# Pairing blocks in the gate's convolution, three common PSUM slots, and a new order of instructions

## The chip, the cores and the metric

The kernel runs on one core of a Trainium2 chip. The metric is the device time of one execution in microseconds (us); lower is better. Three runs of the kernel before gave 912.4, 908.27 and 912.25 us, so the median is 912.25 us. The profile is of one further execution of 914.14 us, whose span from the first to the last instruction is 912.2 us.

The engines are named as in the profile. PE is the matrix engine (TensorE), PEld its weight loads, DVE the vector engine, ACT the scalar engine, POOL is GpSimd, and SP is the engine that issues most of the transfers. PSUM is the memory into which PE writes; here it holds eight banks of 512 fp32 words for each of 128 partitions.

## The reference

The input x has 8 batches of 3200 positions and 256 channels. First comes a filter in the frequency domain, then a gated convolution:

```
X = rfft(x, axis=1);  Xr, Xi = X.real, X.imag
Yr = Xr @ w_r - Xi @ w_i + b_r
Yi = Xr @ w_i + Xi @ w_r + b_i
Yr, Yi = soft_threshold(Yr, 0.01), soft_threshold(Yi, 0.01)
y = irfft(Yr + 1j*Yi, n=3200, axis=1)

gate_pre[:, s] = sum over k of conv_w[k] * y[:, s - 4 + k]     (k = 0..4, zeros ahead of s = 0)
gate = 1 / (1 + exp(-gate_pre))
out  = (gate * (y @ w_val)) @ w_out
```

w_val, conv_w and w_out arrive as 64-bit floats; the kernel turns their bit patterns into fp32 with integer instructions on DVE.

## The kernel before

The transform of length 3200 = 64 x 50 is done as two small matrix products each way. For a batch b the stages are:

- p1 (lines 502 to 579): eight units. Each loads a part of x, multiplies it by a 50-point matrix on PE into a two-bank PSUM tile, adds and subtracts the two halves (a copy on ACT, two operations on DVE, L545 and L551), and stores the result to a scratch tensor in HBM (a_dram).
- p2 (lines 582 to 701) with mixed (703 to 749): six steps of two units and one last step of one unit. Each step loads a part of a_dram, does the 64-point product (s2, L610) into a two-bank PSUM tile, splits it on ACT and DVE into a high and a low part, does the complex product with the weights (L734 and L729, with a sum that DVE writes into PSUM first, called the seed, L738), the soft threshold (ACT L745, DVE L747), and the inverse 64-point product (s1i, L681), and stores to a second scratch tensor (z_dram).
- positions (763 to 808): eight blocks of 400 positions. Each loads a part of z_dram, does the inverse 50-point product (s2i, L787) into a two-bank PSUM tile, and ACT copies it (L794) into y_sb, the one buffer that holds y of a whole batch. Block 7 comes first in every batch, since its last positions are also the ones ahead of block 0 in the layout; three small DVE copies (L800, L806) put them there. It has to wait until the last readers of the batch before are done.
- gated (822 to 887): for each of the eight blocks the values v = y @ w_val (L819 in six fp32r products per half from a high and a low part; or L815 with whole fp32 weights, for the blocks in LATE_VAL), the convolution, the sigmoid, the gate (L861), the output product (L819 or, for the blocks in LATE_OUT, L815), a copy (L885) and the store.

The convolution of one block is done for two channel halves c of 128 channels and 400 positions each. ACT multiplies by the first tap (L846), DVE adds four taps (L849, one scalar_tensor_tensor for each tap and half, each with a [128, 1] operand from cw_sb), and ACT applies the sigmoid in place (L859). In a block of LATE_OUT the output product reads the gated values as they are; in the other blocks ACT and DVE split them first (L332 and L334), and the value product's operand y is split in the same way unless the block is in LATE_VAL.

PSUM is divided as follows: one two-bank slot for the tiles of s2 (tag ps_s2), two two-bank slots that all of p1, s1i, s2i, v and the output product take in turn (tag ps_2), and one bank each for the seed's target (ps_y) and the sum (ps_k).

The order of the instructions is worked out before the launch by the class Plan. Every piece of work is given an engine, a cost, the things it reads and writes, the slots it opens, and a due value `at` (in units: a batch is T = 13). Plan.order then simulates the engines in time. On each engine it takes, among the pieces that could begin within SLACK ns of the earliest, the one of the smallest `at`. What comes out is a fixed order on each engine; the constants in LAND, CLOCK and LANDED (before: a plain 1400) are times that only this simulation uses, and O holds the offsets of the due values. At run time every engine works through its list and waits where an operand or a slot isn't there yet. The slots of one tag are taken in the order of their opening, so the n-th tile of a tag with three slots waits for the last reader of tile n - 3.

Of the kernel before, what the change touches and what calls it, by code (L numbers as in the profile page):

```python
# [11 lines left out]
F32R = mybir.dt.float32r  # L12
# [3 lines left out]
ALU = mybir.AluOpType  # L16
# [76 lines left out]
class Plan:  # L93
# [30 lines left out]
    def order(self):  # L124
# [41 lines left out]
        while len(done) < len(pieces):  # L166
# [71 lines left out]
def act(n, kind="copy"):  # L238
# [7 lines left out]
T = float(NU)  # L246
O = {'spread': -0.013,
     'hold': 0.011,
     'together': 2.151,
     'later': 4.433,  # L250
     'load_x': -2.271,
     'p1': 1.18,
     'p1_step': 1.113,
     'load_a': -3.981,
     's2': -1.406,
     's1i': 1.995,
     'p3': 3.283,
     'load_z': -3.105,
     'y': 0.708,
     'conv': 1.374,  # L260
     'val': 1.657,
     'gate': -2.568,
     'project': 3.372,
     'late_val': 7.023,
     'late_out': 14.484,
     'turn': 0.534,
     'mix_sum': -1.534,
     'p1_1': -0.107,
     'load_x_1': 1.103,
     'p1_2': -1.656,  # L270
     'p3_0': 0.32}
# [9 lines left out]
def fourier_filter_then_gated_conv(ctx: ExitStack, tc: tile.TileContext, x, w_r, w_i, b_r, b_i,  # L281
# [34 lines left out]
    WORDS = {"xs": 3072, "x": 4 * D, "zl": MB * D, "y_hl": 4 * TB, "g_hl": 4 * TB, "s1": 1024, "tp": 2 * D, "o": 2 * TB, "acc": 2 * TB}  # L316

# [4 lines left out]
    def two_banks(key, tag="ps_2"):  # L322
        return buffer(key, tag, [P, 2, 512])
# [112 lines left out]
    def load_bias(at):  # L436
# [15 lines left out]
        def spread():  # L452
            p, q = two_banks(k2, "ps_s2")[:, :, 0:D], buffer(k1, "ps_k", [P, D])
            for k in range(2):
                b = b_sb[0:1, k * D:(k + 1) * D]
                for j in range(2):
                    nc.tensor.matmul(p[:, k, :], m(j), b, start=j == 0, stop=j == 1)
# [44 lines left out]
    def p1(b, u, at):  # L502
# [4 lines left out]
        s_tag = ("s1", "g_hl", "xs")[u % 3] if early else "s1"  # L507
        p_tag = "ps_s2" if early and u % 3 == 2 else "ps_2"
        rows = ROWS if b < 2 else ((0, N2),)
# [72 lines left out]
    def p2(b, d, at):  # L582
# [14 lines left out]
        def s2(i):  # L597
            if i == 0:
                two_banks(k2, "ps_s2")
            if last:  # L600
# [155 lines left out]
    def block(ap):  # L756
        return ap.rearrange("p (h n) -> p h n", h=NH)
# [52 lines left out]
    def matrix(key, e, w, src, whole):  # L810
# [6 lines left out]
        for c in range(2):  # L817
            for hw, hy in ((0, 0), (1, 0), (0, 1)):
                nc.tensor.matmul(p[:, e, 0:TB], w[:, hw, c, e * P:(e + 1) * P], src(hy, c), start=n == 0, stop=n == 5)  # L819
                n += 1  # L820

    def gated(b, k, at):
        bk = (b, k)
        here, there = [("y", k, 0)], [("y", k - 1, j) for j in range(3 if k == 0 else 1)]
        ky, kg, kv, kh, kp, ko = (("y_hl", bk), ("acc", bk), ("v_ps", bk), ("gated", bk), ("o_ps", bk), ("o", bk))
        if bk in LATE_VAL:
# [12 lines left out]

        acc = lambda c: tl[kg][:, c, :]  # L840

        def first(c):
            if c == 0:
                buffer(kg, "acc", [P, 2 * TB])
                tl[kg] = tl[kg].rearrange("p (c n) -> p c n", c=2)
            nc.scalar.mul(block(acc(c)), y_at(k, c, 0), cw_sb[:, c, 0:1])  # L846

        def tap(c, j):
            nc.vector.scalar_tensor_tensor(out=block(acc(c)), in0=y_at(k, c, j), scalar=cw_sb[:, c, j:j + 1],  # L849
                                           in1=block(acc(c)), op0=ALU.mult, op1=ALU.add)  # L850
        for c in range(2):
            add(at + O["conv"] + 0.01 * c, "ACT", act(TB, "conv"), lambda c=c: first(c), [*here, *there, ("cw", 0, 0)],
                [kg + (c,)], {kg: "acc"} if c == 0 else None, chain="conv")
        for j in range(1, KC):
            for c in range(2):
                add(at + O["conv"] + 0.02 * j, "DVE", 61 + dve(TB), lambda c=c, j=j: tap(c, j), [*here, *there], [kg + (c,), *([("turn", "read", (b, c))] if (k, j) == (NB - 1, KC - 1) else [])],
                    delay=545 + (130 if j == KC - 1 else 0))
        for c in range(2):
            add(at + O["conv"] + 0.15, "ACT", act(TB, "sigmoid"), lambda c=c: nc.scalar.activation(  # L859
                out=acc(c), in_=acc(c), func=AF.Sigmoid), (), [kg + (c,)])  # L860
        add(at + O["gate"], "DVE", dve(2 * TB), lambda: nc.vector.tensor_tensor(  # L861
            out=tl[kg], in0=tl[kv][:, :, 0:TB], in1=tl[kg], op=ALU.mult), [kv + (0,), kv + (1,)], [kg + (0,), kg + (1,)])
        if bk in LATE_OUT:
            gs = [kg + (0,), ("w_late", 0, 0)]
            om = lambda e: matrix(kp, e, lambda: w_late[1], lambda h, c: tl[kg][:, c, :], True)
        else:
            gs = [*split(at + O["gate"] + 0.1, 2 * TB, kh, lambda: tl[kg], lambda: tl[kh][:, 0], lambda: tl[kh][:, 1],
                         [kg + (0,)], {kh: "g_hl"}, lambda: buffer(kh, "g_hl", [P, 2, 2, TB], F32R)),
                  ("w", "w_out", "high"), ("w", "w_out", "low")]
            om = lambda e: matrix(kp, e, wo_sb, lambda h, c: tl[kh][:, h, c, :], False)  # L870
# [74 lines left out]
    for b in range(B):  # L945
# [44 lines left out]
```

## Time and profile before

| | us |
|---|---|
| median of three runs | 912.25 |
| profiled execution | 914.14 |
| its span | 912.2 |
| outside the span | 1.9 |
| PE busy / idle within the span | 843.4 / 68.8 |
| DVE busy | 798.9 |
| ACT busy | 584.3 |
| granted TensorE clock, mean | 0.971 |

A group's row gives line, engine, operation, out<-in, shapes and count, then the total busy time in us and the mean of one in ns, then the idle time of the engine ahead of it and what ended it. The mean is that of the instruction alone; instructions of one engine overlap a little, so in a run of like ones the distance from start to start is shorter. A row of waits reads: engine, line of what waited, what it waited for, total us, times, longest us. A row of a timeline gives start and length of a run of like instructions (x count) and, in brackets, the idle time ahead of it.

### The profile page before, as it was taken

What the parts mean: (1) busy time and instruction counts of PE and PEld (TensorE: products, weight loads), DVE (VectorE), ACT (ScalarE), POOL (GpSimd) and SP (SyncE); (2) the same over time, 40 slices, a digit from 0 to 9 for tenths busy, and PEclk for the clock granted to TensorE, in tenths of its full rate; (3) what the DMA queues carried; (4) which work ended last, traced back from release to release, by engine and by line L of the source; (5) the groups of instructions that cost most, each with busy time, mean ns of one, the idle gap of its engine ahead of it and who ended that gap; (6) DMA issues with size and microseconds to landing.
All of it is one profiled execution on the core that took longest, in us unless ns stands there. A gap on an engine that the chain in (4) does not pass through costs nothing.

```text
span 912.2 us, 29342 instructions
## 1 busy us (share of the span) xinstructions
PE 843.4 (92%) x12634; PEld 713.5 (78%) x12634; DVE 798.9 (88%) x1286; ACT 584.3 (64%) x903; POOL 4.5 (0%) x11
## 2 busy tenths in 40 slices
PE   8768988999999997999999998899999999999997
PEld 2356766799788886979888887879887888998774
DVE  2347778999999999899999999799999989999896
ACT  1225444778577774768667775768667667777664
POOL 0000000000000000000000000000001000000000
PEclk9779988999999999999999999999999999999999
DMA  6598986764666647655586647656585445523612
GB/s 170 152 218 210 258 228 207 218 202 131 203 210 205 181 128 239 182 195 157 179 251 210 180 138 238 187 192 169 171 253 183 126 132 171 158 79 107 199 69 78
DMA packets 107220, 163.33 MB, mean 179 GB/s; under 512 B 10302, under 2 KB 80756, under 8 KB 107092
## 3 DMA queue, kind: packets, MB, share of 16 engines
q1 hardware_dynamic: 105332, 158.19, 57.4%
q10 hardware_dynamic: 1760, 3.28, 1.3%
q8 instruction: 99, 1.62, 0.8%
q14 instruction: 29, 0.24, 0.1%
HBM read 82.79 MB, written 78.64 MB: 177 GB/s over the span
## 4 chain that ended last, share of the span: by engine, by line
PE 56%; DVE 20%; DMA 13%; ACT 5%; issue 4%; SPq 2%; ACTq 0%; DVEq 0%
PE y_ps L729 10%; PE v_ps L819 10%; PE o_ps L819 10%; PE z_ps L681 7%; DVE acc L849 6%; PE k_ps L734 5%; PE y_p L787 5%; DMA a_dram<-s 5%; DMA x<-in_x 3%; DVE s L551 3%; PE s L610 3%; DMA zl<-z_dram 2%; PE p L532 2%; DVE y_ps L738 2%; DVE acc L861 2%
## 5 line engine op out<-in xcount | busy, mean ns | idle before, releaser
L849 DVE SCALAR_TENSOR_TENSOR acc<-y_sb,cw_sb,acc 128x400 f32<-128x400 f32 x512 | 297.4, 630 | 1.6 <-ACT acc L846 1.2
L729 PE MATMUL y_ps<-w_sb,xs 128*128 128x256 f32 x1152 | 159.3, 289 | 3.7 <-DVE st_cw L374 2.9
L729 PEld LDWEIGHTS y_ps<-w_sb,xs 128*128 128x128 f32 x1152 | 149.1, 196 | 7.8 <-issue 5.4
L819 PE MATMUL o_ps<-gated,wo_sb 128*128 128x400 f32 x744 | 148.5, 347 | 0.0
L819 PE MATMUL v_ps<-y_hl,wv_sb 128*128 128x400 f32 x660 | 133.1, 348 | 9.4 <-DVE s L551 7.3
L819 PEld LDWEIGHTS o_ps<-gated,wo_sb 128*128 128x128 f32 x744 | 134.6, 188 | 2.4
L819 PEld LDWEIGHTS v_ps<-y_hl,wv_sb 128*128 128x128 f32 x660 | 117.2, 189 | 12.4 <-ACT tp L745 4.8
L551 DVE TENSOR_TENSOR s<-p,s 128x512 f32<-128x512 f32 (+2 forms) x144 | 89.6, 627 | 30.8 <-ACT s L545 16.9
L745 ACT ACTIVATE tp<-y_ps,nlam 128x512 f32<-128x512 f32 (+1 forms) x104 | 69.6, 669 | 69.8 <-PE y_ps L729 67.9
L734 PE MATMUL k_ps<-w_sb,xs 128*128 128x256 f32 x576 | 92.9, 298 | 15.7 <-DVE y_ps L738 13.3
L734 PEld LDWEIGHTS k_ps<-w_sb,xs 128*128 128x128 f32 x576 | 77.3, 193 | 33.5 <-issue 14.3
L681 PE MATMUL z_ps<-tp,g_sb 64*64 64x256 f32 x1536 | 95.0, 380 | 3.0 <-issue 1.7
L747 DVE SCALAR_TENSOR_TENSOR tp<-y_ps,tp 128x512 f32<-128x512 f32 (+1 forms) x104 | 69.2, 665 | 24.1 <-ACT tp L745 23.6
L332 ACT CAST gated<-acc 128x800 fp32r<-128x800 f32 x62 | 53.5, 862 | 53.5 <-DVE acc L861 52.6
L787 PEld LDWEIGHTS y_p<-g_sb,zl 50*64 50x64 f32 x4096 | 67.6, 137 | 25.0 <-issue 13.2
L787 PE MATMUL y_p<-g_sb,zl 50*64 50x50 f32 x4096 | 73.0, 221 | 11.9 <-issue 9.4
L846 ACT ACTIVATE acc<-y_sb,cw_sb 128x400 f32<-128x400 f32 x128 | 75.8, 626 | 7.1 <-DVE gated L334 6.2
L610 PEld LDWEIGHTS s<-f_sb,a 64*64 64x64 f32 x3072 | 59.2, 139 | 26.9 <-issue 17.1
L681 PEld LDWEIGHTS z_ps<-tp,g_sb 64*64 64x64 f32 x1536 | 57.3, 133 | 28.9 <-issue 6.7
L532 PE MATMUL p<-x,f_sb 50*64 50x512 f32 x256 | 73.1, 662 | 3.4 <-DMA x<-in_x 2.3
L859 ACT ACTIVATE acc<-acc 128x400 f32<-128x400 f32 x128 | 66.8, 538 | 12.0 <-DVE acc L849 11.8
L794 ACT COPY y_sb<-y_p 128x800 f32<-128x800 f32 x64 | 52.9, 827 | 32.2 <-PE y_p L787 32.0
(80 smaller groups left out, 1046.5 us busy)
## 6 DMA issues: line engine op xcount, KB each, us to landing
zl<-z_dram SPq DMA_DIRECT2D x128, 200.0 KB
out<-o SPq DMA_DIRECT2D x63, 400.0 KB
a<-a_dram SPq DMA_DIRECT2D x96, 256.0 KB
z_dram<-z_t SPq DMA_DIRECT2D x48, 512.0 KB
x<-in_x SPq DMA_DIRECT2D x90, 200.0 KB
a_dram<-s SPq DMA_DIRECT2D x90, 200.0 KB
x<-in_x SPq DMA_DIRECT2D x23, 192.0 KB
a_dram<-s SPq DMA_DIRECT2D x15, 192.0 KB
```

The costliest lines, as they stand in the source:

```text
L532: nc.tensor.matmul(p[k * HP:(k + 1) * HP, 0, :], f1_sb[half(0), 0:HP], xt[half(0), k * 512:(k + 1) * 512], start=True, stop=True)
L551: nc.vector.tensor_tensor(out=st()[lo:hi, h, n], in0=tl[kp][lo:hi, 0, n], in1=st()[lo:hi, 1, n], op=(ALU.add, ALU.subtract)[h])
L610: nc.tensor.matmul(p[e * HP:(e + 1) * HP, h, c, t, :], tl[ka][rows, t, c * P + e * HP:c * P + (e + 1) * HP], f2_sb[rows, (4 * d + t) * N1: ...
L681: nc.tensor.matmul(p[e * HP:(e + 1) * HP, i, j * D:(j + 1) * D], g[i * HP:(i + 1) * HP, r, e * HP:(e + 1) * HP], tl[kts[j]][i * HP:(i + 1) ...
L729: nc.tensor.matmul(p[:, 1 - r, :], xm(hx, c, r, i), w_sb[:, m, hw, c, :], start=False, stop=k == 5, skip_group_check=True)
L734: nc.tensor.matmul(p, sm(hx, c, i), w_sb[:, 0, hw, c, :], start=k == 0, stop=k == 5)
L745: nc.scalar.activation(out=buffer(kt, "tp", [P, 2, D])[:, 0:n], in_=tl[ky][:, 0:n], func=AF.Relu, bias=nlam)
L747: add(at + 0.2, "DVE", dve(n * D), lambda: nc.vector.scalar_tensor_tensor(out=tl[kt][:, 0:n], in0=tl[ky][:, 0:n], scalar=LAM, in1=tl[kt][: ...
L787: nc.tensor.matmul(pv[h][e * HP:(e + 1) * HP, c, m, :], zt[half(h), m, c * P + e * HP:c * P + (e + 1) * HP], g2_sb[half(h), :], start=True ...
L819: nc.tensor.matmul(p[:, e, 0:TB], w[:, hw, c, e * P:(e + 1) * P], src(hy, c), start=n == 0, stop=n == 5)
L846: nc.scalar.mul(block(acc(c)), y_at(k, c, 0), cw_sb[:, c, 0:1])
L849: nc.vector.scalar_tensor_tensor(out=block(acc(c)), in0=y_at(k, c, j), scalar=cw_sb[:, c, j:j + 1], in1=block(acc(c)), op0=ALU.mult, op1=A ...
```

## The change

Three things change.

1. The tag ps_s2 is gone. The tiles of s2 (and one tile for spreading the bias at the start) are opened under ps_2, which has three slots instead of two.
2. The convolution moves out of gated into a function conv of its own that works on a pair of neighbouring blocks. One ACT instruction multiplies 800 positions by the first tap where there were two of 400; one DVE instruction adds a tap over 800; one ACT sigmoid runs over 800. The pair's accumulator has four times TB words and two buffers (before: two times TB, two buffers). The gate, the split, the products and the stores stay one per block and read their half of the pair's accumulator.
3. The offsets in O, and with them the order, are new; so are the simulation's constants. Two of the offsets set which blocks use whole fp32 weights: late_val goes from 7 to 5 (of 16 listed blocks: batch 6 and 7) and late_out from 14 to 7, so the value products of two more blocks and the output products of seven more blocks use L815's form and need no split.

```diff
-LAND = {"PE": 215, "DVE": 130, "ACT": 150, "POOL": 200, "SP": 0}
+LAND = {"PE": 260, "DVE": 180, "ACT": 200, "POOL": 200, "SP": 0}
+LANDED = 2500
...
-     'later': 4.433,
-     'load_x': -2.271,
+     'later': 32.5466,
+     'load_x': -2.7464,
...
-     's2': -1.406,
+     's2': 0.159,
...
-     'load_z': -3.105,
-     'y': 0.708,
-     'conv': 1.374,
-     'val': 1.657,
-     'gate': -2.568,
-     'project': 3.372,
-     'late_val': 7.023,
-     'late_out': 14.484,
+     'load_z': -11.5153,
+     'y': 4.3699,
+     'conv': 2.4499,
+     'val': 4.0492,
+     'gate': 1.0849,
+     'project': 4.6284,
+     'late_val': 5.023,
+     'late_out': 7.02,
...
-     'load_x_1': 1.103,
+     'load_x_1': 53.3967,
...
-         "acc": 2, "g_hl": 2, "o": 2, "ps_s2": 1, "ps_y": 1, "ps_k": 1, "ps_2": 2, "a_dram": 2, "z_dram": 2}
+         "acc": 2, "g_hl": 2, "o": 2, "ps_y": 1, "ps_k": 1, "ps_2": 3, "a_dram": 2, "z_dram": 2}
...
-                two_banks(k2, "ps_s2")
+                two_banks(k2, "ps_2")
...
+    def conv(b, kk, at):
+        k = 2 * kk
+        here, there = [("y", k, 0), ("y", k + 1, 0)], [("y", k - 1, j) for j in range(3 if k == 0 else 1)]
...
+        w = 2 * MB * N2
+        acc = lambda c: tl[kg][:, c]
+        wide = lambda c, j: y_sb[:, c, :, (k * MB + j) * N2:(k * MB + j) * N2 + w]
...
+            nc.scalar.mul(acc(c), wide(c, 0), cw_sb[:, c, 0:1])
...
+            nc.vector.scalar_tensor_tensor(out=acc(c), in0=wide(c, j), scalar=cw_sb[:, c, j:j + 1], in1=acc(c), op0=ALU.mult, op1=ALU.add)
...
+            add(at + O["conv"] + 0.15, "ACT", act(2 * TB, "sigmoid"), lambda c=c: nc.scalar.activation(
+                out=acc(c), in_=acc(c), func=AF.Sigmoid), (), [kg + (c, e) for e in range(2)])
...
         add(at + O["gate"], "DVE", dve(2 * TB), lambda: nc.vector.tensor_tensor(
-            out=tl[kg], in0=tl[kv][:, :, 0:TB], in1=tl[kg], op=ALU.mult), [kv + (0,), kv + (1,)], [kg + (0,), kg + (1,)])
+            out=part(), in0=by_half(tl[kv][:, :, 0:TB]), in1=part(), op=ALU.mult), [kv + (0,), kv + (1,)], ours)
...
-            if i:
-                gated(b, k, start + (i - 1) * T / NB)
+            if i and i % 2 == 0:
+                conv(b, k // 2, start + (i - 1) * T / NB)
+                gated(b, i - 2, start + (i - 2) * T / NB)
+                gated(b, i - 1, start + (i - 1) * T / NB)
```

More of the change, by code (lines that the diff above doesn't have):

```diff
@@ L314, in buffer @@
         return tl[key]
-    WORDS = {"xs": 3072, "x": 4 * D, "zl": MB * D, "y_hl": 4 * TB, "g_hl": 4 * TB, "s1": 1024, "tp": 2 * D, "o": 2 * TB, "acc": 2 * TB}
+    WORDS = {"xs": 3072, "x": 4 * D, "zl": MB * D, "y_hl": 4 * TB, "g_hl": 4 * TB, "s1": 1024, "tp": 2 * D, "o": 2 * TB, "acc": 4 * TB}
     def room(key, tag, words, dtype=F32):
@@ L507, in p1 @@
         s_tag = ("s1", "g_hl", "xs")[u % 3] if early else "s1"
-        p_tag = "ps_s2" if early and u % 3 == 2 else "ps_2"
+        p_tag = "ps_2"
         rows = ROWS if b < 2 else ((0, N2),)
@@ L820, in matrix, with first, tap @@
                 n += 1
+    def conv(b, kk, at):
+        k = 2 * kk
+        here, there = [("y", k, 0), ("y", k + 1, 0)], [("y", k - 1, j) for j in range(3 if k == 0 else 1)]
+        kg = ("acc", (b, kk))
+        w = 2 * MB * N2
+        acc = lambda c: tl[kg][:, c]
+        wide = lambda c, j: y_sb[:, c, :, (k * MB + j) * N2:(k * MB + j) * N2 + w]
+        def first(c):
+            if c == 0:
+                tl[kg] = room(kg, "acc", 4 * TB).rearrange("p (c h n) -> p c h n", c=2, h=NH)
+            nc.scalar.mul(acc(c), wide(c, 0), cw_sb[:, c, 0:1])
+        def tap(c, j):
+            nc.vector.scalar_tensor_tensor(out=acc(c), in0=wide(c, j), scalar=cw_sb[:, c, j:j + 1], in1=acc(c), op0=ALU.mult, op1=ALU.add)
+        for c in range(2):
+            add(at + O["conv"] + 0.01 * c, "ACT", act(2 * TB, "conv"), lambda c=c: first(c), [*here, *there, ("cw", 0, 0)],
+                [kg + (c, e) for e in range(2)], {kg: "acc"} if c == 0 else None, chain="conv")
+        for j in range(1, KC):
+            for c in range(2):
+                add(at + O["conv"] + 0.02 * j, "DVE", 61 + dve(2 * TB), lambda c=c, j=j: tap(c, j), [*here, *there],
+                    [*[kg + (c, e) for e in range(2)], *([("turn", "read", (b, c))] if (kk, j) == (NB // 2 - 1, KC - 1) else [])],
+                    delay=961 + (130 if j == KC - 1 else 0))
+        for c in range(2):
+            add(at + O["conv"] + 0.15, "ACT", act(2 * TB, "sigmoid"), lambda c=c: nc.scalar.activation(
+                out=acc(c), in_=acc(c), func=AF.Sigmoid), (), [kg + (c, e) for e in range(2)])
     def gated(b, k, at):
         bk = (b, k)
-        here, there = [("y", k, 0)], [("y", k - 1, j) for j in range(3 if k == 0 else 1)]
-        ky, kg, kv, kh, kp, ko = (("y_hl", bk), ("acc", bk), ("v_ps", bk), ("gated", bk), ("o_ps", bk), ("o", bk))
+        here = [("y", k, 0)]
+        ky, kg, kv, kh, kp, ko = (("y_hl", bk), ("acc", (b, k // 2)), ("v_ps", bk), ("gated", bk), ("o_ps", bk), ("o", bk))
         if bk in LATE_VAL:
@@ L837, in gated @@
                 {kv: "ps_2"} if e == 0 else None, chain="val")
[L840 to L857, printed above, removed]
@@ L858, in gated @@
-        for c in range(2):
-            add(at + O["conv"] + 0.15, "ACT", act(TB, "sigmoid"), lambda c=c: nc.scalar.activation(
-                out=acc(c), in_=acc(c), func=AF.Sigmoid), (), [kg + (c,)])
+        ours = [kg + (c, k % 2) for c in range(2)]
+        part = lambda: tl[kg][:, :, :, (k % 2) * MB * N2:(k % 2 + 1) * MB * N2]
+        by_half = lambda ap: ap.rearrange("p c (h n) -> p c h n", h=NH)
         add(at + O["gate"], "DVE", dve(2 * TB), lambda: nc.vector.tensor_tensor(
-            out=tl[kg], in0=tl[kv][:, :, 0:TB], in1=tl[kg], op=ALU.mult), [kv + (0,), kv + (1,)], [kg + (0,), kg + (1,)])
+            out=part(), in0=by_half(tl[kv][:, :, 0:TB]), in1=part(), op=ALU.mult), [kv + (0,), kv + (1,)], ours)
```

42 lines of the change are left out of this document (21 added, 21 removed).

## The prediction

> **What bounds the kernel now.** I read the engines' busy times first:
>
> ```profile
> PE 843.4 (92%) x12634; PEld 713.5 (78%) x12634; DVE 798.9 (88%) x1286; ACT 584.3 (64%) x903; POOL 4.5 (0%) x11
> ```
>
> PE is busy for 843.4 of 912.2 us, DVE for 798.9. Neither can shrink much below its own work, so the question is where PE's 68.8 us of idle time lie. Three stretches (columns: length; busy us of PE, PEld, DVE, ACT, POOL; granted clock; DMA share; GB/s):
>
> ```profile
> 0.00:160.00 160.00, 129.96 (x1531) 88.04 (x1532) 94.77 (x167) 59.10 (x93) 1.15 (x9) 0.88 0.78 206
> 160.00:850.00 690.00, 658.72 (x10428) 586.40 (x10427) 653.58 (x1037) 488.41 (x754) 3.38 (x2) 0.99 0.58 179
> 850.00:912.20 62.20, 54.67 (x680) 39.03 (x678) 50.59 (x84) 36.81 (x57) 0.00 (x0) 0.96 0.32 110
> ```
>
> The start (first p1 and p2) leaves PE idle for 30.0 us. In the middle, where p1, p2, positions and gate of neighbouring batches are interleaved, PE is 95.5% and DVE 94.7% busy: two nearly full engines in fixed orders that wait for one another, with 31.3 us idle. The end, gate work alone, has 7.5 us. PE's waits in the three stretches say which idle time the change can reach. The middle:
>
> ```profile
> PE y_p L787 <- issue: 9.4, 4, 2.8
> PE v_ps L819 <- DVE s L551: 7.3, 6, 1.7
> PE k_ps L734 <- DVE y_ps L738: 7.0, 12, 1.6
> PE s L610 <- issue: 2.4, 2, 1.4
> PE v_ps L819 <- ACT tp L745: 1.7, 1, 1.7
> PE z_ps L681 <- issue: 1.7, 1, 1.7
> ```
>
> Of the 31.3 us, 13.5 (9.4 + 2.4 + 1.7) are "issue": PE waited for nothing that the profile shows, some in the middle of a run of products, and no part of the change touches that. 7.3 are a slot: the value product reads nothing of p1, so what it waits for in L551 is the two-bank slot that L551 empties. 7.0 are DVE's backlog: the seed L738 comes late, and ps_k isn't free for the next sum. With the 1.7 for ACT L745 that makes 16.0 that lighter engines and a third slot could reach. The start:
>
> ```profile
> PE k_ps L734 <- DVE y_ps L738: 6.3, 7, 2.1
> PE bias L457 <- DVE s L551: 5.2, 1, 5.2
> PE s L610 <- DVE xs L659: 3.5, 1, 3.5
> PE y_ps L729 <- DVE st_cw L374: 2.9, 1, 2.9
> PE k_ps L734 <- DVE xs L663: 2.4, 1, 2.4
> ```
>
> And the end, where three short waits are for a slot that the gate L861 empties:
>
> ```profile
> PE y_p L787 <- DVE acc L861: 2.1, 3, 1.1
> PE v_ps L815 <- DVE acc L861: 1.0, 1, 1.0
> ```
>
> **The change part by part: the pairs.** The costs come from these groups and from DVE's timeline near the end:
>
> ```profile
> L849 DVE SCALAR_TENSOR_TENSOR acc<-y_sb,cw_sb,acc 128x400 f32<-128x400 f32 x512 | 297.4, 630 | 1.6 <-ACT acc L846 1.2
> L659 DVE TENSOR_TENSOR xs<-s,xs 128x1024 fp32r<-128x1024 f32 x48 | 58.3, 1215 | 0.0
> L663 DVE TENSOR_TENSOR xs<-sx,xs 128x512 fp32r<-128x512 f32 x48 | 32.8, 683 | 0.0
> L846 ACT ACTIVATE acc<-y_sb,cw_sb 128x400 f32<-128x400 f32 x128 | 75.8, 626 | 7.1 <-DVE gated L334 6.2
> L859 ACT ACTIVATE acc<-acc 128x400 f32<-128x400 f32 x128 | 66.8, 538 | 12.0 <-DVE acc L849 11.8
> ```
> ```profile
> 898.82 0.99 DVE L861 TENSOR_TENSOR acc<-v_ps,acc 128x800 f32<-128x800 f32 x1
> 899.72 3.36 DVE L849 SCALAR_TENSOR_TENSOR acc<-y_sb,cw_sb,acc 128x400 f32<-128x400 f32 x6
> ```
>
> Six taps take 3.36 us, the last of them 0.63, so one follows another after (3.36 - 0.63) / 5 = 0.546 us. An element costs (1215 - 683) / 512 = 1.04 ns on DVE, so a tap over 800 costs 0.546 + 400 x 0.00104 = 0.962. No row shows such a tap; its bounds are the gate over 800, from 898.82 to 899.72 = 0.90, and two single taps, 1.09. I take 0.962, which the row of the same operation gives. A pair of taps saves 0.13 us, and 256 pairs save 33 us of DVE (0 to 49 by the bounds). On ACT an element's price isn't needed to the digit: with the same 1.04 as an upper bound a first tap over 800 is at most 0.626 + 0.42 = 1.04 us, and a sigmoid 0.95, so 64 of each at most cost 128 us against 75.8 + 66.8 = 142.6 now. ACT, at 64%, isn't a bound and I give that no time of its own.
>
> The Trainium skill (VectorE: DVE Perf Modes, "The TRN2 errata") has a fixed cost per instruction too, but 58 cycles at 0.96 GHz for SBUF operands, 60 ns. By that the pairs would save 256 x 0.06 = 15 us of DVE, not 33, the seed term below would be about half, and the forecast about 900. Here the trace disagrees: 0.546 us less 400 x 1.04 ns leaves 130 ns, and I go by it.
>
> **Late blocks.** Nine more product pairs use whole weights. PE's timeline shows both kinds:
>
> ```profile
> 579.91 2.35 PE L819 MATMUL v_ps<-y_hl,wv_sb 128*128 128x400 f32 x12
> 582.10 1.56 PE L729 MATMUL y_ps<-w_sb,xs 128*128 128x256 f32 x12
> ```
> ```profile
> 879.36 2.64 PE L819 MATMUL o_ps<-gated,wo_sb 128*128 128x400 f32 x12
> 881.84 2.85 PE L815 MATMUL v_ps<-y_sb,w_late 128*128 128x400 f32 x8
> 884.22 2.64 PE L819 MATMUL o_ps<-gated,wo_sb 128*128 128x400 f32 x12
> 887.52 1.15 PE L787 MATMUL y_p<-g_sb,zl 50*64 50x50 f32 x64 [0.67 <-DVE acc L861]
> ```
>
> An L819 block takes 582.10 - 579.91 = 2.19 us. One L819 and one L815 take 884.22 - 879.36 = 4.86, so L815 costs 4.86 - 2 x 2.19 = 0.48 more. Nine cost 4.3 us of PE: three in batch 6 (1.4 in the middle) and six in batch 7 (2.9 in the end). They spare DVE nine subtractions of 0.90 (8.1 us) and ACT nine casts. Together DVE goes from 798.9 to 798.9 - 33 - 8 = 758 us. About 29 + 3 us of that fall in the middle, so DVE's share there goes from 94.7% to (653.6 - 32) / 690 = 90%.
>
> **The middle.** The three slots: by the code 39 tiles a batch go through two slots now and 46 through three afterwards. L713 runs once a batch,
>
> ```profile
> L713 DVE COPY y_ps<-bias_sb x8: 419/421/428, 124.1 to 829.9; 128x256 f32<-128x256 f32 x8
> ```
>
> so a batch takes 705.8 / 7 = 100.8 us, and a tile may hold its slot for 2 x 100.8 / 39 = 5.2 us now and 3 x 100.8 / 46 = 6.6 us afterwards before it delays anyone. A fold of p1 that comes late then has 1.4 us more, against waits of 1.7 at the longest; I count the 7.3 us as gone (bounds: all gone, or 7 more where a tile of s2, which two casts and two subtractions must read, holds up the ring). Of the seed's 7.0 I take half, 3.5, since DVE's spare time doubles from 5.3% to 10%; of the 1.7 on ACT 1.0. With the late blocks the middle gets -7.3 - 3.5 - 1.0 + 1.4 = -10.4 us. What a new order does to the other work on PE has no row: from +5 to -5.
>
> **The start.** No pair's work lies there. 'later' 32.5 puts the float conversions (L374 and its neighbours) behind all other DVE work that is ready: the 2.9 and 2.4 us above, both behind them, should go. If they slip past need, the first value product waits, at 0.4 to 0.7 us for each step. 'load_x_1' puts batch 1's loads of x last on SP; what is queued behind each is a store or a load of scratch, which then goes earlier, and who may wait instead is p1 of batch 1, PE's filler of eight units. The three tags of batch 0's p1 become three slots of one tag, which is the same. The s2 tile need no longer wait for L659 (3.5). I take -5 of the 8.8 us, with bounds of -12 and +8. SP's other moves (load_z earlier) cost nothing while the loads wait for the batch's last store; three buffers cover them, and without that cover a load's landing would show in front of L787. POOL has nothing that moves.
>
> **The end.** The third slot takes the 3.1 us. The late blocks add 2.9. The last pair adds to the chain behind the last y_p (887.52): its eight taps take 8 x 0.962 against 8 x 0.546, 3.3 us, and first tap and sigmoid about 0.35 each; products of the blocks before can cover that, and I charge 2, with bounds 0 and 6. Sum -3.1 + 2.9 + 2 = +1.8.
>
> **The sum.** 914.1 - 10.4 - 5 + 1.8 = 900.5 us for an execution like the profiled one, span 912.2 with 1.9 around it. The median lies 1.9 below that execution, so I say 898.5. The likeliest case by itself reaches from 888 to 907.
>
> **The rivals.** *More goes than I think.* All 16.0 of the middle, the 20.3 of the start's rows and the 3.1 vanish, and only the late blocks' 4.3 come back: 912.25 - 35.1 = 877; with the bias wait of 5.2 left, which no edit touches, 882. For it: DVE is behind in nearly every wait that isn't "issue". Against it: these waits are different events, and a static order seldom loses them all.
>
> *It doesn't do what it says.* The third slot is only the old s2 slot renamed: s2 tiles hold theirs longest, the next tiles in the ring wait behind them, the 7.3 stay, and DVE's spared time becomes DVE's idle time behind "issue". Then -3.5 - 1.0 + 1.4 in the middle, 0 in the start and +4 at the end: 913. Against it stands the 1.4 us of slack just worked out.
>
> *The turn of the batch decides (slower).* Between two batches DVE has few taps to do already:
>
> ```profile
> 569.38 0.70 DVE L738 TENSOR_TENSOR y_ps<-k_ps,bias_sb 128x512 f32<-128x512 f32 x1
> 573.12 0.99 DVE L334 TENSOR_TENSOR y_hl<-y_sb,y_hl 128x800 fp32r<-128x800 f32 x1 [3.04 <-ACT y_hl L332]
> 574.03 2.27 DVE L849 SCALAR_TENSOR_TENSOR acc<-y_sb,cw_sb,acc 128x400 f32<-128x400 f32 x4
> ```
>
> It sits idle for 3.04 us and starts on block 0 at 574.03. A pair must also wait for block 1: a y_p of 1.15 us on PE, a copy and a longer first tap, some 2 us, unless the taps of block 1 were to wait that long anyway. If nothing fills it and the products behind the gate come late by as much, PE loses 2 us at each of 7 turns, 14; nothing is won in the middle but the slot or the seed (-4), and the late blocks and the last pair cost 4.3 + 4: 912.25 + 18 = 930. It decides once DVE's idle time at a turn passes some 5 us. Against it: p2 of the next batch is there to fill in.
>
> *The clock falls at the turns.* A wait of 3.5 us ahead of L610 fell in this slice:
>
> ```profile
> 50.00:60.00 10.00, 6.62 (x96) 5.09 (x97) 5.47 (x8) 5.59 (x9) 0.00 (x0) 0.66 0.97 221
> ```
>
> where PE got 0.66 of its clock. If the turns open such a gap, each costs 3.5 us and about 10 x (1 - 0.66) = 3.4 us of slow clock on top: 7 x 6.9 = 48, about 960. By a rule of the Trainium skill (TensorE: Matmul & The Clock Gate, "HAM oscillation") gaps of over some 3.4 us throttle PE; the slice agrees. Today's longest wait in the middle is 2.8.
>
> **How the numbers follow.** Forecast 0.48, more goes 0.16, doesn't do what it says 0.16, turn 0.17, clock 0.03. A range of 882 to 920 leaves out about half of the second case, 0.08, and 0.12 of the last two. A median of this kernel can be told from no change at about 0.5%, 4.6 us: faster is below 907.7, which takes the forecast and the second case, 0.64; same is the third, 0.16; slower is the rest, 0.20.
>
> **What would show it.** L849 in 256 instructions over 800 with about 0.96 us from one to the next; DVE busy about 758, PE about 848. The row of L819 waiting for L551 gone from the middle and the row of the seed halved, "issue" as it was; L713 about 99 us apart. No PE wait for L374 in the start, and none for x of batch 1. I am wrong if the middle's idle time is no smaller with DVE at 90%, if DVE's idle time gathers at the turns, or if the start gets longer.

## The result, and the profile after

Four runs of the changed kernel took 884.45, 881.42, 891.55 and 881.38 us, a median of 882.93, against 910.6 us for four runs of the kernel before (908.27 to 912.4). The ratio is 0.9717 with a 95% interval of 0.9647 to 0.9787: the change takes 2.8% off. The forecast was 898.5, the range 882 to 920.

The page of the changed kernel begins with its engines' busy times, in the same columns as before:

```profile
span 882.6 us, 28987 instructions
PE 836.6 (95%) x12598; PEld 695.9 (79%) x12598; DVE 756.7 (86%) x1021; ACT 554.6 (63%) x766; POOL 4.5 (1%) x11
```

DVE did 756.7 us of work, against 758 forecast. PE did 836.6 instead of the 848 forecast, and that in a span of 882.6. The lines of the changed kernel are one higher than before up to L788 (the seed is L739, the fold of p1 L552), the products of the gate are L820 and L816, the tap is L837, the first tap L834, the sigmoid L847 and the gate L871. The tap's group and two of its runs in DVE's timeline:

```profile
L837 DVE SCALAR_TENSOR_TENSOR acc<-y_sb,cw_sb,acc 128x800 f32<-128x800 f32 x256 | 261.0, 1049 | 14.9 <-ACT acc L834 14.5
```
```profile
334.75 2.97 DVE L837 SCALAR_TENSOR_TENSOR acc<-y_sb,cw_sb,acc 128x800 f32<-128x800 f32 x3
...
867.19 2.97 DVE L837 SCALAR_TENSOR_TENSOR acc<-y_sb,cw_sb,acc 128x800 f32<-128x800 f32 x3
```

There are 256 of them, and one follows another after (2.97 - 1.05) / 2 = 0.96 us, which is the price that the prediction worked out.

To see where the time went, cut both traces at the same event, the copy that runs once a batch (L713, now L714). Its row after, and the stretches ahead of the first one, between first and last, and behind the last one, of the kernel before and then of the changed one:

```profile
L714 DVE COPY y_ps<-bias_sb x8: 416/420/428, 126.3 to 799.2; 128x256 f32<-128x256 f32 x8
```
```profile
0.00:124.10 124.10, 99.27 (x952) 63.43 (x956) 66.51 (x119) 41.31 (x65) 1.15 (x9) 0.88 0.80 204
124.10:829.90 705.80, 669.80 (x10884) 593.86 (x10877) 662.61 (x1054) 493.58 (x761) 3.38 (x2) 0.99 0.59 182
829.90:912.20 82.30, 74.28 (x804) 56.18 (x802) 69.81 (x115) 49.43 (x77) 0.00 (x0) 0.97 0.33 114
```
```profile
0.00:126.30 126.30, 102.01 (x1100) 61.28 (x1104) 68.65 (x116) 43.66 (x70) 1.15 (x9) 0.84 0.77 210
126.30:799.20 672.90, 655.15 (x10726) 582.83 (x10719) 629.46 (x843) 470.41 (x648) 3.30 (x2) 0.99 0.61 189
799.20:882.60 83.40, 79.42 (x782) 51.80 (x780) 58.57 (x66) 40.55 (x50) 0.00 (x0) 0.99 0.34 117
```

| stretch | before | after | difference | of it PE idle, before and after |
|---|---|---|---|---|
| ahead of the first L713 / L714 | 124.1 | 126.3 | +2.2 | 24.8, 24.3 |
| seven batches between | 705.8 | 672.9 | -32.9 | 36.0, 17.8 |
| behind the last | 82.3 | 83.4 | +1.1 | 8.0, 4.0 |

The whole gain lies in the seven batches between: 96.1 us from one to the next instead of 100.8. There PE went from 94.9% to 97.4% busy. DVE did 33 us less and the stretch got 33 us shorter, so DVE's share hardly moved (93.9% and 93.5%). PE's work there fell by 14.7 us; 2.7 more lie in the start and 5.1 more in the end, and the rest, 6.8, is less busy time in all. The two groups that fell most are the short products L734 (now L735: 92.9 to 87.6 us) and L610 (L611: 61.5 to 56.2); some others grew.

PE's waits in the middle stretch of the changed kernel, counted from 160 to 820 us:

```profile
PE y_p L788 <- issue: 7.3, 7, 1.8
PE k_ps L735 <- DVE y_ps L739: 3.4, 1, 3.4
PE o_ps L820 <- DVE s L552: 0.8, 2, 0.5
PE y_ps L730 <- DVE y_ps L739: 0.8, 3, 0.4
PE v_ps L820 <- DVE s L552: 0.6, 1, 0.6
```

The wait for the slot that the fold of p1 holds is 1.4 us (0.8 + 0.6) instead of 7.3, the wait for the seed 4.2 (3.4 + 0.8) instead of 7.0, and "issue" 7.3 instead of 13.5. The fall of the seed's wait hangs on where the stretch is cut, though. Between the copies of L713 and L714, where the gain lies, the rows of PE for the seed and for L663 were, before and then after,

```profile
PE k_ps L734 <- DVE y_ps L738: 8.8, 15, 1.6
PE k_ps L734 <- DVE xs L663: 2.4, 1, 2.4
PE y_ps L729 <- DVE y_ps L738: 0.9, 1, 0.9
```
```profile
PE k_ps L735 <- DVE y_ps L739: 5.0, 3, 3.4
PE y_ps L730 <- DVE y_ps L739: 3.2, 5, 1.9
```

so the seed went from 9.7 us to 8.2 only. Of the 18.2 us of idle time that PE lost there, 6.4 are "issue" (13.7 to 7.3), 5.9 the slot of p1's fold (7.3 to 1.4), 2.4 the wait for L663, 1.7 the one for ACT L745, and 1.5 the seed.

For the last 62 us the view has no wait of PE at all. The start still waits for the seed, and longer than before for a load of scratch (5.1 us against 2.6); its largest rows up to 160 us:

```profile
PE k_ps L735 <- DVE y_ps L739: 10.6, 8, 3.6
PE s L611 <- DMA a<-a_dram: 5.1, 4, 2.9
PE y_ps L730 <- DVE y_ps L739: 4.1, 4, 1.9
PE p L533 <- ACT s L546: 3.9, 3, 2.8
```

### The profile page after: what moved, and what is told of

The parts are those of the page before. It is cut to its first block, busy times and chain, and to the rows that moved or that the text cites. A ratio compares the mean times of both kernels' runs of the same rounds, so it can differ in the third digit from the quotient of the medians.

```text
span 882.6 us, 28987 instructions
## 1 busy us (share of the span) xinstructions
PE 836.6 (95%) x12598; PEld 695.9 (79%) x12598; DVE 756.7 (86%) x1021; ACT 554.6 (63%) x766; POOL 4.5 (1%) x11
## 4 chain that ended last, share of the span: by engine, by line
PE 76%; DVE 11%; DMA 6%; issue 3%; ACT 2%; SPq 1%; ACTq 0%; DVEq 0%
PE y_ps L730 14%; PE o_ps L820 13%; PE v_ps L820 12%; PE z_ps L682 7%; PE y_p L788 7%; PE k_ps L735 7%; PE s L611 4%; PE p L533 4%; PE v_ps L816 3%; DVE acc L837 3%; DMA x<-in_x 3%; PE o_ps L816 3%; DMA a_dram<-s 2%; DVE y_ps L739 2%; DVE s L552 2%
## 5 line engine op out<-in xcount | busy, mean ns | idle before, releaser
L837 DVE SCALAR_TENSOR_TENSOR acc<-y_sb,cw_sb,acc 128x800 f32<-128x800 f32 x256 | 261.0, 1049 | 14.9 <-ACT acc L834 14.5
L730 PEld LDWEIGHTS y_ps<-w_sb,xs 128*128 128x128 f32 x1152 | 145.9, 191 | 24.8 <-DVE y_ps L739 11.0
L730 PE MATMUL y_ps<-w_sb,xs 128*128 128x256 f32 x1152 | 159.1, 288 | 4.9 <-DVE y_ps L739 4.7
L820 PE MATMUL o_ps<-gated,wo_sb 128*128 128x400 f32 x660 | 132.6, 348 | 1.0 <-DVE s L552 0.8
L820 PE MATMUL v_ps<-y_hl,wv_sb 128*128 128x400 f32 x636 | 126.5, 347 | 0.6 <-DVE s L552 0.6
L820 PEld LDWEIGHTS o_ps<-gated,wo_sb 128*128 128x128 f32 x660 | 117.2, 188 | 6.0 <-issue 1.8
L820 PEld LDWEIGHTS v_ps<-y_hl,wv_sb 128*128 128x128 f32 x636 | 113.2, 188 | 1.3 <-ACT xs L656 0.8
L552 DVE TENSOR_TENSOR s<-p,s 128x512 f32<-128x512 f32 (+2 forms) x144 | 89.1, 627 | 27.1 <-ACT s L548 14.3
L735 PE MATMUL k_ps<-w_sb,xs 128*128 128x256 f32 x576 | 87.6, 289 | 14.1 <-DVE y_ps L739 14.0
L735 PEld LDWEIGHTS k_ps<-w_sb,xs 128*128 128x128 f32 x576 | 79.1, 194 | 23.0 <-issue 11.5
L748 DVE SCALAR_TENSOR_TENSOR tp<-y_ps,tp 128x512 f32<-128x512 f32 (+1 forms) x104 | 69.2, 665 | 23.0 <-ACT tp L746 22.2
L895 ACT COPY o<-o_ps 128x800 f32<-128x800 f32 x63 | 52.0, 825 | 45.5 <-PE o_ps L820 33.6
L533 PE MATMUL p<-x,f_sb 50*64 50x512 f32 x256 | 74.4, 669 | 6.3 <-ACT s L546 3.9
L788 PEld LDWEIGHTS y_p<-g_sb,zl 50*64 50x64 f32 x4096 | 66.5, 135 | 17.4 <-issue 11.2
L788 PE MATMUL y_p<-g_sb,zl 50*64 50x50 f32 x4096 | 72.7, 220 | 7.5 <-issue 7.3
L540 PE MATMUL p<-x,f_sb 50*64 50x512 f32 x240 | 75.0, 673 | 0.0
L847 ACT ACTIVATE acc<-acc 128x800 f32<-128x800 f32 x64 | 55.5, 873 | 25.2 <-DVE acc L837 24.7
L611 PEld LDWEIGHTS s<-f_sb,a 64*64 64x64 f32 x3072 | 53.0, 136 | 22.0 <-issue 15.4
L333 ACT CAST y_hl<-y_sb 128x800 fp32r<-128x800 f32 x53 | 45.6, 863 | 39.0 <-PE v_ps L820 38.5
```

Of the source, the lines that this page charges most:

```text
L533: nc.tensor.matmul(p[k * HP:(k + 1) * HP, 0, :], f1_sb[half(0), 0:HP], xt[half(0), k * 512:(k + 1) * 512], start=True, stop=True)
L540: nc.tensor.matmul(dst, f1_sb[half(1), 0:HP], back[:, 2 * k:2 * k + 2, :], start=True, stop=True)
L552: nc.vector.tensor_tensor(out=st()[lo:hi, h, n], in0=tl[kp][lo:hi, 0, n], in1=st()[lo:hi, 1, n], op=(ALU.add, ALU.subtract)[h])
L611: nc.tensor.matmul(p[e * HP:(e + 1) * HP, h, c, t, :], tl[ka][rows, t, c * P + e * HP:c * P + (e + 1) * HP], f2_sb[rows, (4 * d + t) * N1: ...
L730: nc.tensor.matmul(p[:, 1 - r, :], xm(hx, c, r, i), w_sb[:, m, hw, c, :], start=False, stop=k == 5, skip_group_check=True)
L735: nc.tensor.matmul(p, sm(hx, c, i), w_sb[:, 0, hw, c, :], start=k == 0, stop=k == 5)
```

## The experiments

The first question was whether the 33 us taken off DVE make the gain (relief), whatever the order, or the new order, or the slots. Two kinds of run answer it. In the first kind nothing but the length of DVE's taps changes, so every engine's list of instructions keeps its order: in the traces of these runs DVE and ACT go through the same instructions, one after the other, as in the kernel that they start from, but for the doubled taps of the second. In the second kind a part of the change is taken alone or undone, and the order is laid out anew by the same simulation. Each run was timed against the kernel before; a ratio is that of the two.

### The order kept, DVE's taps lighter or heavier

**The kernel before with lighter taps.**

```diff
-            nc.vector.scalar_tensor_tensor(out=block(acc(c)), in0=y_at(k, c, j), ...
-                                           in1=block(acc(c)), op0=ALU.mult, op1=ALU.add)
+            n = 169
+            nc.vector.scalar_tensor_tensor(out=block(acc(c))[:, :, 0:n], in0=y_at(k, c, j)[:, :, 0:n], ...
+                                           in1=block(acc(c))[:, :, 0:n], op0=ALU.mult, op1=ALU.add)
```

> The kernel before in its own order, but each tap covers 338 of its 400 positions (the convolution is incomplete), so that 512 taps cost DVE about 62 x 1.04 = 64 ns less each, 33 us in all, as much as the pairs save. Nothing else changes, on any engine. If DVE's load is what sets the pace (relief theory), the waits for the seed and for the late fold shrink at once: 912 - 8 to - 18, so 894 to 904. If the old order has its waits built in and the gain needs an order laid out for the shorter work (order theory), it moves by under 4 us: 907 to 912.

Ratio 0.9939 (0.9903 to 0.9976), median 908.2 us. Its row of the copy that runs once a batch:

```profile
L713 DVE COPY y_ps<-bias_sb x8: 418/420/428, 122.5 to 827.2; 128x256 f32<-128x256 f32 x8
```

DVE's busy time fell by 27.5 us (798.9 to 771.4), somewhat less than the 33 meant. Seven batches take 704.7 us, against 705.8. In the order of before, the relief is worth 1 us there, and 0.6% in all. Between the copies PE is as idle as before (35.3 us against 36.0): its wait for L551 fell from 7.3 us to 3.2, and waits for ACT (2.9 for L545 and 2.1 for the sigmoid) and a little more "issue" stand in its place. The median lies where the order theory put it, though it moved by 5 us (from 913.47 in the same series) and not by under 4.

**The changed kernel with two taps over 400 in place of one over 800.**

```diff
-            nc.vector.scalar_tensor_tensor(out=acc(c), in0=wide(c, j), scalar=cw_sb[:, c, j:j + 1], in1=acc(c), ...)
+            n = MB * N2
+            for e in range(2):
+                part = slice(e * n, (e + 1) * n)
+                nc.vector.scalar_tensor_tensor(out=acc(c)[:, :, part], in0=wide(c, j)[:, :, part], ...
+                                               in1=acc(c)[:, :, part], op0=ALU.mult, op1=ALU.add)
```

> The changed kernel in its own order, slots and blocks, but each tap over 800 is issued as two over 400 one behind the other, which gives DVE its 33 us back (256 x 0.13) and nothing else. Relief theory: DVE is over 95% busy between the markers again, and most of the 28 us is lost: 900 to 912. Order theory: the order and slots keep most of the gain, and the time rises by under 10 us: 884 to 893.

Ratio 0.9951 (0.9918 to 0.9983), median 909.12 us: of the 2.8% only 0.5% is left. Its stretches at the same cuts:

```profile
0.00:127.20 127.20, 99.66 (x1100) 61.34 (x1104) 68.62 (x117) 43.78 (x70) 1.15 (x9) 0.88 0.77 209
127.20:819.50 692.30, 658.10 (x10743) 582.08 (x10737) 656.04 (x1056) 471.38 (x648) 3.33 (x2) 1.00 0.60 184
819.50:905.40 85.90, 79.05 (x770) 50.70 (x762) 63.81 (x107) 40.25 (x50) 0.00 (x0) 0.99 0.32 109
```

With the same order, slots and blocks, 27 us more of DVE (656.0 against 629.5) make the seven batches 19.4 us longer (692.3 against 672.9), and PE's idle time there goes from 17.8 to 34.2. The relief theory's number came out (900 to 912); the order by itself doesn't hold the gain. ACT's shorter work and the late blocks are still in this run, so without the lighter taps they don't make the gain either.

**The changed kernel with lighter taps still.**

```diff
-            ... out=acc(c), in0=wide(c, j), scalar=cw_sb[:, c, j:j + 1], in1=acc(c), ...
+            ... out=acc(c)[:, :, 0:338], in0=wide(c, j)[:, :, 0:338], scalar=cw_sb[:, c, j:j + 1], in1=acc(c)[:, :, 0:338], ...
```

> The changed kernel in its own order, but each tap covers 338 of 400 positions of each half (the convolution is incomplete), which takes another 256 x 0.13 = 33 us off DVE. If DVE's load still sets part of the pace: PE's remaining waits for DVE go (some 17 us of idle time in the start for the seed L739, 9.6 in the middle): 865 to 877. If PE is now the bound and its waits are built into the order: 879 to 884.

Ratio 0.9681 (0.9625 to 0.9737), median 883.49 us: not to be told from the changed kernel's 0.9717.

```profile
L714 DVE COPY y_ps<-bias_sb x8: 416/419/428, 125.8 to 796.1; 128x256 f32<-128x256 f32 x8
```
```profile
PE 832.8 (95%) x12598; PEld 695.0 (79%) x12598; DVE 730.3 (83%) x1021; ACT 554.7 (63%) x766; POOL 4.3 (0%) x11
```

Another 26 us off DVE (730.3) shorten the seven batches by 2.6 us (670.3). So in the new order the time follows DVE's work from 788 us down to 757, and from 757 to 730 it doesn't. PE, 97.5% busy between the cuts in this run, is then the likely bound, but no run makes PE's work in these batches lighter. The 17 and 9.6 us that the expectation names are also more than PE's rows for the seed in the changed kernel, 18.7 us in all.

### Parts of the change, with an order of their own

**Offsets and constants alone**, on single blocks and the old slots:

```diff
-LAND = {"PE": 215, "DVE": 130, "ACT": 150, "POOL": 200, "SP": 0}
+LAND = {"PE": 260, "DVE": 180, "ACT": 200, "POOL": 200, "SP": 0}
-                delay = wire - start + 1400 + p["extra"]
+                delay = wire - start + 2500 + p["extra"]
-O = {'spread': -0.013, ...
+O = {'spread': -0.5666, ...
```

> The kernel before with single blocks and the old slots (one for s2, two for the rest), but with the changed kernel's offsets O (late blocks included) and its simulation's constants. Order theory: most of the gain is here, 885 to 898. Relief theory: the nine late blocks' 8 us of DVE are all the relief there is, and offsets made for pairs fit single blocks badly: 905 to 925.

Ratio 1.051 (1.0450 to 1.0571), median 959.03: slower by far more than either theory had it.

**Pairs and slots with the offsets and constants of before:**

```diff
-O = {'spread': -0.5666, ...
+O = {'spread': -0.013, ...
-LAND = {"PE": 260, "DVE": 180, "ACT": 200, "POOL": 200, "SP": 0}
+LAND = {"PE": 215, "DVE": 130, "ACT": 150, "POOL": 200, "SP": 0}
-LANDED = 2500
+LANDED = 1400
```

> The changed kernel's pairs and three slots, with the offsets O (late blocks as before) and the constants of the kernel before. Relief theory: DVE has its 33 us less and the slot is there, so most of the gain is here, 885 to 898. Order theory: under a third of it, 903 to 915.

Ratio 1.1057 (1.1008 to 1.1107), median 1009.87, far outside both expectations. PE's waits between 160 and 820 us:

```profile
PE k_ps L735 <- DVE y_ps L739: 35.9, 25, 3.4
PE y_p L788 <- issue: 13.3, 5, 4.1
PE o_ps L820 <- ACT gated L333: 12.8, 5, 2.6
PE y_ps L730 <- DVE y_ps L739: 9.0, 5, 3.7
```

PE waits most for the seed, and the output product waits for the gate's split. A pair is complete only with its second block, but this order asks for the gate as if each block came alone. That this is the reason is a reading, which the next run tests.

**The same with five of the changed offsets**, those of the gate's work:

```diff
-     'y': 0.708,
-     'conv': 1.374,
-     'val': 1.657,
-     'gate': -2.568,
-     'project': 3.372,
+     'y': 4.3699,
+     'conv': 2.4499,
+     'val': 4.0492,
+     'gate': 1.0849,
+     'project': 4.6284,
```

> Pairs and three slots with the offsets of the kernel before, as in the run of 1009.9 us, but with five offsets of the changed kernel: y, conv, val, gate and project, which put the gate's work 1.1 to 3.7 units later. If the old offsets fail because they ask for the gate's product before its pair can be ready (the first block of a pair is complete only with the second, 13 / 8 = 1.6 units later), these five bring most of it back: 885 to 925. If the loss lies in the rest of the order (p1, p2, loads), it stays near 1000.

Ratio 1.0287 (1.0214 to 1.0361), median 941.23. That is 69 us less than without them and 58 more than the changed kernel. Between the copies of L714 the output product's wait for ACT L333, 12.8 us, is gone, and that of L735 for the seed went from 41.4 us to 22.8. The reason given for the old offsets' failure fits, but the five don't bring the time into the expected 885 to 925.

**The three slots alone** (the kernel before with the slots of the changed one):

```diff
-         ... "ps_s2": 1, "ps_y": 1, "ps_k": 1, "ps_2": 2, ...
+         ... "ps_y": 1, "ps_k": 1, "ps_2": 3, ...
```

> The kernel before with the three common slots alone: single blocks, its own offsets and constants, so that the order is laid out anew only as far as the slots allow. If the slot was a bound of its own, the 7.3 us of waits for L551 go: 903 to 908. If the slot counts only together with the rest (order theory), anything that isn't a gain: 908 to 930, since these offsets were made for one s2 slot apart.

Ratio 1.0382 (1.0314 to 1.0449), median 950.15, slower than either expectation has it. PE's largest row is now the seed's, 24.7 us.

**The changed kernel with the old slots** (the same lines the other way round):

> The changed kernel with one slot for s2 and two for the rest again; pairs, offsets and constants as changed. If the third slot carries 7 us as the prediction has it: 888 to 895, with waits of L820 for L552 back. If the offsets fit only the slots that they were made for: over 900, spread over many waits. If the slots are worth nothing: 881 to 887.

Ratio 1.0317 (1.0259 to 1.0374), median 942.85. Two of its largest rows of waits, over the whole span, are waits for slots:

```profile
PE s L611 <- DVE xs L660: 9.8, 4, 3.5
PE y_p L788 <- DVE acc L871: 8.4, 2, 4.8
```

L611 reads nothing that L660 writes, nor L788 anything of L871; L660 empties the one slot of s2, and L871 one of the other two. So this order does run into the slots, for 18 us at least; the other 40 us or so of its 60 over the changed kernel are elsewhere.

**The late blocks as before:**

```diff
-     'late_val': 5.023,
-     'late_out': 7.02,
+     'late_val': 7.023,
+     'late_out': 14.484,
```

> The changed kernel with nine blocks of whole fp32 value weights and two of output weights, as before the change, instead of eleven and nine. By the prediction's prices PE does 4.3 us less and DVE 8.1 us more, most of it in the last two batches. If PE is what the end waits for, the time falls by 2 to 4 us: 879 to 881. If DVE's and ACT's splits in the end cost more than that: 884 to 892.

Ratio 0.9735 (0.9669 to 0.9801), median 887.88: no difference to the changed kernel that can be told. PE's busy time is 830.7 us and DVE's 764.5, that is 5.9 less and 7.8 more than in the changed kernel, near the 4.3 and 8.1 of the prediction's prices.

**'later' and 'load_x_1' as before:**

```diff
-     'later': 32.5466,
-     'load_x_1': 53.3967,
+     'later': 4.433,
+     'load_x_1': 1.103,
```

> The changed kernel with 'later' and 'load_x_1' as in the kernel before (the float conversions and batch 1's loads of x early again). The prediction's start term of -5 us says the stretch up to the first L714 gets longer, from 126.3 to some 131. The traces of before and after (124.1 and 126.3) rather say that these two offsets win nothing there: 121 to 127 for the stretch. For the whole time 880 to 892 unless the order behind the start suffers, which would show as a longer distance from batch to batch than 96.1 us.

Ratio 1.0079 (1.0039 to 1.0120), median 920.74.

```profile
L714 DVE COPY y_ps<-bias_sb x8: 417/419/421, 134.5 to 832.4; 128x256 f32<-128x256 f32 x8
```

The start is 8.2 us longer (134.5 against 126.3), more than either expectation has it, so in this setting the two offsets do shorten it. But 25 us more come from the seven batches (697.9 against 672.9), on which neither offset has a direct hold. That raised the question of what any new order costs.

### What a new order costs by itself

**One offset moved by 0.1**, in the changed kernel and in the kernel before:

```diff
-     'p3': 3.5438,
+     'p3': 3.6438,
```
```diff
-     'p3': 3.283,
+     'p3': 3.383,
```

> The changed kernel with one offset moved by a little: p3, the due value of all of positions and gate, 3.5438 to 3.6438, 0.1 units or some 0.75 us later. Pairs, slots and work are the same; only the order differs. If the single order matters less than what the work is, 880 to 890. If every order laid out anew loses a few per cent against the one that was chosen, 900 to 930, and then the runs that changed slots or late blocks with a new order say little about slots and late blocks.

> The same shift of p3 by 0.1 in the kernel before (3.283 to 3.383). If the order of before is no better than its neighbours, 908 to 918; if any new order loses, 925 to 950, as the run with three slots alone (950.2) would then have to be read.

The changed kernel goes to 1.0099 (1.0062 to 1.0135), median 920.21; the kernel before to 1.0199 (1.0087 to 1.0312), that is by some 18 us, with a wide interval. The work, the pairs and the slots are those of the unshifted kernels. Of the shifted changed kernel, the copy that runs once a batch and PE's three largest rows of waits over the whole span:

```profile
L714 DVE COPY y_ps<-bias_sb x8: 415/418/428, 128.2 to 836.7; 128x256 f32<-128x256 f32 x8
```
```profile
PE y_ps L730 <- DVE y_ps L739: 17.7, 14, 1.9
PE k_ps L735 <- DVE y_ps L739: 14.7, 9, 4.5
PE o_ps L820 <- DVE s L552: 8.0, 5, 1.7
```

The seven batches take 708.5 us, 35.6 more than in the unshifted one, and the waits for the seed are 32.4 us (17.7 + 14.7) where the changed kernel has 18.7 (14.0 + 4.7, the groups of L735 and L730 on its page). The third row is the wait for the slot of p1's fold: 8.0 us, against 0.8 in the changed kernel, with the same three slots. So with the very same work one order or the next makes 37 us by the medians, which come from two series, and 3.8% by the ratios (1.0099 against 0.9717): more than the whole change.

This settles how the second kind of run is to be read. The slots alone, the old slots in the changed kernel, the five offsets and the start's offsets each came with an order of their own, and in the two kernels where it was tried an order by itself moved the time by some 18 and 37 us. None of these runs prices its part. The late blocks are another matter: in that run's trace DVE's instructions are those of the changed kernel up to the 960th of 1021, at 797 us, so its order is new in the end alone, and it says that the late blocks are worth nothing that can be told. What stands besides are the runs that kept the order: in the old one 27.5 us of DVE's busy time are worth 0.6%; in the new one 31.8 us (788.5 to 756.7) are worth 2.3 of the 2.8 points, and another 26.4 nothing that can be told.

## Why the prediction was right or wrong

The direction and the range held; the forecast of 898.5 was 15.6 us too high. The time fell by 27.7 us where the sum has 13.75, and the range held by 0.9 us: its lower end, 882, is the number of the rival "More goes than I think" and doesn't come from the sum, so it held by luck. By its steps:

- **The pairs' price.** 0.962 us a tap was forecast and 0.96 measured; DVE's 758 us against 756.7. Right.
- **The middle, -10.4.** Measured -32.9 us between the cuts at L713. This is the step that failed, in size. The prediction added up the waits of PE that the trace put down to DVE, ACT and slots, 16.0 us, and took some of that as all that could come. Its slot term held in the rows (7.3 to 1.4). The half of the seed's came true in the prediction's own stretch (7.0 to 4.2), but between the copies the seed fell by 1.5 us only (9.7 to 8.2). Above all, the rows of waits weren't the bound on the gain: "issue", which no part of the change was to touch, fell by half as well, PE's busy time fell by 6.8 us where +4.3 was forecast, and PE's work moved into the start and the end. The run with two taps over 400 shows the coupling that the sum left out: in one order, 27 us of DVE are 19 us of time. The step "DVE's share there goes from 94.7% to 90%" was wrong in the same way: it divided by the old length. DVE's share stayed at 93.5% as the stretch shrank with it.
- **That the relief works at once** wasn't said, but the term for the seed supposed that waits shrink with DVE's load in whatever order. With the old order and lighter taps, the seven batches gained 1 us. The relief was worth its time in the chosen order. That an order is laid out for the lighter work isn't enough: that of the shifted kernel was too, and it took 920.21 us.
- **The order's own effect, "from +5 to -5".** Far too narrow: 0.1 on one offset moved the changed kernel by 37 us and the kernel before by some 18 (2.0%, with an interval of 0.9 to 3.1).
- **The start, -5.** Measured +2.2; a longer start was one of the signs by which the prediction called itself wrong. The waits for the conversions (L374) and for L663 behind them did go, and no row of PE up to 160 us waits for L660, which L659 has become; a longer one for a load of scratch (5.1 against 2.6) and a new one for ACT L546 (3.9) stand in their place, and the seed's row went from 6.3 us to 10.6, with 4.1 more ahead of L730 (0.9 before). The waiting moved rather than went. The 5.2 us for the bias, which the prediction held that no edit touches, went too; the slots alone aren't the reason, since the run with them alone still has 4.7. Putting the two offsets back made the start 8.2 us longer, but in another order.
- **The end, +1.8.** Measured +1.1, at other cuts. The waits for the gate's slot are gone, as said. A block of L816 in the end takes 870.40 - 867.71 = 2.69 us,

```profile
867.71 2.85 PE L816 MATMUL o_ps<-acc,w_late 128*128 128x400 f32 x8
870.40 2.85 PE L816 MATMUL v_ps<-y_sb,w_late 128*128 128x400 f32 x8
```

  0.50 more than the 2.19 of an L819 block, against 0.48 forecast.
- **The rivals.** "More goes than I think" gave 882, and 882.9 was measured, but not by its account, in which the start loses 15 of its 20.3 us of waits. "It doesn't do what it says" and the turn of the batch fell: DVE's idle time at a turn stayed under the 5 us that the rival names (2.3 to 3.4 us at each of six turns, from 5 us ahead of the copy L801 to 10 behind it; up to 4.0 before), and the batches follow one another faster than before. The clock in the seven batches stayed at 0.99 on average, and no gap of 3.5 us, as the rival on the clock has it, opened at the turns. From 160 us on it did fall in them for some 3.4 us at a time, though, and behind shorter waits than the 3.4 us that the prediction names: three times in the kernel before, behind waits of PE of 2.75, 1.64 and 1.90 us, and twice in the changed one, behind 1.80 and 3.40 us. The stretches of the kernel before and then of the changed one:

```profile
364.60:368.00 3.40, 3.40 (x127) 3.40 (x127) 0.56 (x1) 2.27 (x4) 0.00 (x0) 0.51 0.50 171
705.90:709.30 3.40, 3.40 (x18) 3.40 (x17) 2.78 (x4) 1.72 (x3) 0.00 (x0) 0.52 0.52 146
733.20:736.60 3.40, 3.35 (x26) 3.26 (x27) 0.95 (x2) 0.83 (x1) 0.00 (x0) 0.52 0.79 241
```
```profile
164.90:168.30 3.40, 3.40 (x47) 3.40 (x50) 1.44 (x5) 0.83 (x1) 0.00 (x0) 0.51 0.32 90
188.70:192.20 3.50, 3.47 (x16) 3.47 (x17) 3.50 (x4) 2.01 (x3) 0.00 (x0) 0.51 0.74 231
```

  Waits of 2.34 us (to 570.85) and 2.43 us (to 775.91) in the kernel before were not followed by one, so these traces give no length from which a wait slows PE.

What is still open: how much the third slot is worth by itself, since no run took it away and kept the order; why PE's code came late less often (below) and why the busy time of L735 and L611 fell; and what the chosen order has that its neighbour, 37 us slower, has not, beyond fewer waits for the seed and for the slot of p1's fold.

## What to carry to other kernels

Here two engines were both near 95% busy in fixed orders, and the waits that the trace put down to one of them were no upper bound on what lighter work on it was worth; a run that only makes its instructions shorter or longer, with the order kept, measures that in one step, and tells when the other engine takes over. The lighter work paid in the one order that was chosen with it and hardly in the old one, and undoing one part of such a change and laying out the whole order again prices the order more than the part. Move an offset that should not matter by a little first: here that alone made 2 to 4%.

## What the runs showed that was not expected

- A DVE instruction's fixed cost depends on its operands. The tap, with its [128, 1] operand, takes 0.96 - 800 x 0.00104 = 0.13 us from start to start over what its elements take, at 800 as at 400. A subtraction over 800 without such an operand, in DVE's timeline of the kernel before,

```profile
179.12 0.98 DVE L334 TENSOR_TENSOR gated<-acc,gated 128x800 fp32r<-128x800 f32 x1
180.02 0.98 DVE L861 TENSOR_TENSOR acc<-v_ps,acc 128x800 f32<-128x800 f32 x1
```

  is followed after 180.02 - 179.12 = 0.90 us, that is 0.07 over its elements. The operation has little to do with it: L748 is a scalar_tensor_tensor too, with a plain number as its scalar, and in the changed kernel,

```profile
312.17 0.68 DVE L748 SCALAR_TENSOR_TENSOR tp<-y_ps,tp 128x512 f32<-128x512 f32 x1
312.77 1.04 DVE L837 SCALAR_TENSOR_TENSOR acc<-y_sb,cw_sb,acc 128x800 f32<-128x800 f32 x1
```

  it is followed after 0.60 us, 0.07 over its 512 elements. The 58 cycles (60 ns) of the Trainium skill (VectorE: DVE Perf Modes, "The TRN2 errata") are near the subtraction's 0.07; for the tap the measured 0.13 decides.
- A shift of one due value by 0.1 units, under 1 us, moved the kernel before by some 18 us and the changed one by 37, with all work unchanged.
- In the kernel before, 23 us less of DVE's busy time in the seven batches (662.6 to 639.6) left their distance as it was (100.7 us against 100.8); in the changed one, 26.6 (656.0 to 629.5) moved it from 98.9 to 96.1.
- By the times in the trace, "issue" was PE waiting for its own code. The page lists a queue that brings instructions, before

```profile
q8 instruction: 99, 1.62, 0.8%
```

  or 99 packets of 16 KB, one for every 255 of PE's 25,268 products and weight loads. The trace has the times of each. This wait of PE in the kernel before,

```profile
364.60 1.71 PE L787 MATMUL y_p<-g_sb,zl 50*64 50x50 f32 x57 [2.75 <-issue]
```

  ended 1.46 us after such a packet, under way from 362.15 to 363.14, had landed. The same holds for all seven of PE's waits on "issue" in the kernel before and all six in the changed one (of 0.2 us or more, from 40 us on): each ends 1.3 to 1.6 us after a packet's landing. Of PE's other waits 4 of 42 and 2 of 24 end 1.1 to 1.7 us after one. So this idle time isn't fixed: it moves with the order, by which packets land too late.
